# A gated mix of chunked attention and a SwiGLU network on one core: weight squares gathered in every third unit, block operands stored in pairs, the second half's operands elsewhere, and the first scan spread out

## The chip, the cores and the metric

The kernel is one launch on one core of a Trainium2 chip. The metric is device time in microseconds (us), the median of several executions. The core's engines run side by side, each with its own queue of instructions in program order: PE multiplies matrices (PEld loads its weights), DVE, ACT and POOL do elementwise work, and SP only issues DMAs. Every DMA of this kernel is issued by SP, in program order. An engine waits at an instruction until what it reads is written and until the buffer that it writes has been released by its last reader.

## The reference, cut

```python
x: [1, 2048, 576]                        # S = 2048 tokens, D = 576, 32 heads of 18, F = 4608
q, k, v = x @ wq, x @ wk, x @ wv         # four segments of 512 tokens
for s in range(4):                       # causal softmax attention inside the segment,
    a_dot = softmax(q_s @ k_s.T * 18 ** -0.5 + mask) @ v_s
    a_mem = (phi(q_s) @ M) / (phi(q_s) @ z + 1e-6)      # and a memory of the earlier ones
    o_s = sigmoid(beta) * a_mem + (1 - sigmoid(beta)) * a_dot
    M, z = M + phi(k_s).T @ v_s, z + phi(k_s).sum()
a = concat(o) @ wo
b = (silu(x @ w_gate) * (x @ w_up)) @ w_down
g = sigmoid((x * gate_w).sum(-1))
out = g * a + (1 - g) * b
```

All inputs and outputs are float32.

## The kernel before

**Two stages and a tail.** Stage one (0 to 234 us) computes q, k, v and the memory for the four segments: in each segment nine chains of matmuls for q and k (line 173), then eight v steps. Counted over the stage, chain n of segment s is step 17 s + n and v step n is step 17 s + 9 + n. Each chain has a list of small pieces of work for the other engines (`mid`), put between its matmuls. Stage two (234 to 1690 us) is the feed-forward network, with the attention's softmax woven in. The tail multiplies by `wo` and mixes.

**Units and beats.** Stage two runs over 72 units: half 0 is units 0 to 35 and half 1 is units 36 to 71. A half is half of the tokens (first segments 2 and 3, then 0 and 1), and a unit is one of 36 tiles of 128 of the 4608 columns, in both the gate and the up projection. The two projections of a unit are done in seven block products (a fast 2x2 block product that needs seven and not eight; `seven`, lines 1181 and 1184) whose operands are sums and differences of blocks of the weights and of x. Each operand is multiplied by a power of two and split into a float16 high part (by ACT, scale and copy) and a low part (by DVE, scale and subtract the high part): three products high x high, high x low, low x high. Line 1184 adds the last 64 rows of D, called the rest. ACT's copy at line 1249 takes the first product out of its bank. After the first four products there is one beat each, after the fifth also (beat 4), two after the sixth (beats 5 and 6), and one after the seventh (beat 7). `defer(k, fn)` puts a piece of work into the k-th beat from now; the work of one beat is issued in the order in which it was deferred.

**Long and short units.** The down projection (line 993) is done for three units together: with the first unit of each next three (units 3, 6, 9, ...) come sixteen groups of matmuls, spread over its beats together with the attention steps. These units are long (some 37 us of PE work); the others are short (10.6 us). An attention step is a generator (`att_gen`): it loads a row and four q and k stacks (lines 246 and 936), multiplies q and k for the row maxima (line 823, maxima at 830), later multiplies again and takes the exponential (lines 870 and 874), masks on POOL (882), rounds to float16 on DVE (960), takes the remainder on POOL (962) and multiplies with v (899, 901).

**Scales.** The power of two of x and of each group of four weight tiles comes from a scan of the data: `peak` on DVE (line 136, the largest square) or `square` on ACT (line 133, the sum of squares), one column of `sc` per tile; then `total` sums the columns, `power` turns them into a power of two, and `back` keeps its inverse. x and the first two weight groups are scanned in stage one: x in segment 0 (`scan`, `scan_step`), the 16 gate and up tiles of groups 0 and 1 in segment 1 (`look`), with the rests in segments 1 and 2. The other seven groups are scanned in half 0 by `glance`: a tile of 128x640 is loaded into a slot of x that half 1 will use, and squared by ACT eight beats later. Two or three glances belong to each of units 0 to 20, long or short; the last total and power come in unit 22.

**Weights.** `w_load` brings a unit's raw gate and up blocks two units ahead, in beats 2 and 5, into one of four buffers called raw (lines 252 to 257). `w_make` (297 to 324) makes the seven operands of the next unit: four sums on POOL (`total`), seven high parts on ACT (line 309), seven low parts on DVE (312), and seven stores (`keep`) to a DRAM tensor `wc`, from which half 1 fetches them (`w_fetch`).

**The second half's x.** Half 1 needs its own x operands: `rest_second` loads and splits the rest rows (DVE at line 199, ACT at 198) in units 30 and 31; `x_second` loads eight pieces of x, forms eight differences on POOL and makes fourteen splits (ACT line 129, DVE line 130), in the last two units of half 0 and in the ten beats behind them. The exponential and the silu need different tables on ACT: `exp_table` (lines 1174 and 1266) switches back, and the two silu instructions of a unit (lines 1274 and 1275 multiply with their results) switch to the other.

## Time and profile before

| What | Value |
|---|---|
| three runs | 1790.54, 1792.91, 1794.20 us (median 1792.91) |
| the profiled execution | 1789.5 us, of which the span is 1787.8 |
| granted clock of PE, mean over the span | 0.997 |
| PE busy | 1739.2 us (97%), 12401 matmuls |
| PE weight loads | 1228.8 us (overlap with PE) |
| DVE busy | 1359.4 us (76%) |
| ACT busy | 1021.7 us (57%) |
| POOL busy | 841.1 us (47%) |
| DMA | 290.21 MB, 162 GB/s on average |

The span runs from the first to the last instruction; the remaining 1.7 us lie around it. A busy time is the union of the instructions on an engine, in one profiled execution. In the rows by time, a row begins with its start and its duration in us, then engine, line and operation, output and inputs by the names of the program, shapes, and in brackets how long the engine stood idle before it and on what. In the rows by stretch, each engine has its busy time and, in brackets, its count of instructions. The share of a whole engine hides that the stages have different limits; the stretches are therefore cut at the starts of units, which are 234.2 (unit 0), 269.6 (3), 325.2 (6), 388.0 (9), 448.6 (12), 632.7 (21), 691.7 (24), 749.9 (27), 808.2 (30), 875.3 (33) and 955.6 us (36, the first of half 1).

### The profile page before, as it was taken

Reading aid. Unit: us, or ns where it says so; the run is one execution under the profiler, and the core shown is the slowest. Engines: PE = TensorE matmul, PEld = TensorE weight load, DVE = VectorE, ACT = ScalarE, POOL = GpSimd, SP = SyncE. Lnnn points to the kernel's source line nnn. Section 1 sums busy time; section 2 is a strip of 40 time slices with the busy share of each in tenths; the row PEclk is TensorE's granted clock in tenths of the full one; section 3 lists DMA queues with packets and bytes.
Section 4 is the critical chain, followed back from the end, with each engine's and each line's share of the span. In section 5 each row is a group of like instructions: output and inputs, shape, how many; then the busy total and the mean of one; then the engine's idle time right before and its main releaser. Section 6 shows DMA issues by size and latency. Waiting matters only on the chain.

```text
span 1787.8 us, 36760 instructions
## 1 busy us (share of the span) xinstructions
PE 1739.2 (97%) x12401; PEld 1228.8 (69%) x12401; DVE 1359.4 (76%) x3447; ACT 1021.7 (57%) x1848; POOL 841.1 (47%) x1065
## 2 busy tenths in 40 slices
PE   8999999999999999999999999999999999999999
PEld 6898856656755676666566757756766766766699
DVE  7678676778878878887877887778778778775455
ACT  6666585676577667655665555455455455465411
POOL 3335541345534544454444555555555555556121
PEclk9999999999999999999999999999999999999999
DMA  8745485775577555645555353354344344333544
GB/s 289 257 172 172 149 288 163 220 234 175 171 230 234 158 178 177 195 124 159 162 154 186 105 153 108 94 153 126 91 134 135 104 120 141 104 107 115 169 147 140
DMA packets 259933, 290.21 MB, mean 162 GB/s; under 512 B 91488, under 2 KB 204000, under 8 KB 259744
## 3 DMA queue, kind: packets, MB, share of 16 engines
q1 hardware_dynamic: 259744, 287.86, 52.0%
q8 instruction: 98, 1.61, 0.4%
q14 instruction: 91, 0.75, 0.2%
HBM read 189.94 MB, written 97.81 MB: 161 GB/s over the span
## 4 chain that ended last, share of the span: by engine, by line
PE 75%; DVE 9%; ACT 6%; DMA 5%; issue 4%; SPq 1%; POOL 1%; DVEq 0%; ACTq 0%; POOLq 0%
PE bank L1181 26%; PE bank L993 23%; PE bank L173 9%; PE bank L1184 4%; PE bank L870 4%; PE bank L823 4%; PE bank L899 2%; DMA xo<-in_wf_dram 1%; PE bank L901 1%; ACT xo L133 1%; DVE row L1274 1%; DVE row L1275 1%; DVE scr L830 1%; ACT bank L1249 1%; PE bank L481 1%
## 5 line engine op out<-in xcount | busy, mean ns | idle before, releaser
L993 PE MATMUL bank<-dw,hh 128*128 128x320 f32 (+1 forms) x2304 | 507.6, 313 | 7.0 <-DVE ya L1002 5.9
L962 POOL TENSOR_TENSOR p<-pe,p 128x512 f16<-128x512 f32 x320 | 380.1, 1188 | 183.1 <-DVE p L960 132.0
L993 PEld LDWEIGHTS bank<-dw,hh 128*128 128x128 f32 x2304 | 378.4, 189 | 33.2 <-DVE ya L1002 9.0
L874 ACT ACTIVATE pe<-bank 128x512 f32<-128x512 f32 x320 | 190.1, 594 | 338.6 <-PE bank L870 306.5
L993 PE MATMUL bank<-dw,hl 128*128 128x320 f32 (+1 forms) x1152 | 340.1, 295 | 0.2 <-DVE hl L126 0.2
L882 POOL TENSOR_SCALAR_AFFINE_SELECT pe<-pe 128x256 f32<-128x256 f32 (+1 forms) x320 | 146.0, 456 | 247.8 <-ACT pe L874 246.2
L830 DVE CUSTOM_DVE_ANT_0 scr<-bank,cm 128x512 bf16<-128x512 f32 (+3 forms) x512 | 247.6, 484 | 18.3 <-PE bank L823 9.3
L1002 DVE TENSOR_TENSOR ya<-bank,ya 128x320 f32<-128x320 f32 x352 | 156.6, 452 | 89.3 <-PE bank L993 86.9
L993 PEld LDWEIGHTS bank<-dw,hl 128*128 128x128 f32 x1152 | 217.6, 189 | 0.5 <-DVE hl L126 0.4
L1184 PE MATMUL bank<-xr,rh 128*128 128x512 f16 x504 | 191.3, 380 | 0.5 <-DMA rh<-rc 0.5
L870 PE MATMUL bank<-qst,kst 111*128 111x512 bf16 (+3 forms) x512 | 151.2, 303 | 0.0
L960 DVE CAST p<-pe 128x512 f16<-128x512 f32 x320 | 149.2, 467 | 0.0
L1092 DVE TENSOR_TENSOR hl<-row,hh 128x512 fp32r<-128x512 f32 x120 | 110.4, 920 | 26.0 <-ACT hh L1091 26.0
L823 PE MATMUL bank<-kst,qst 108*128 108x512 bf16 (+3 forms) x512 | 125.9, 299 | 2.5 <-ACT pe L874 1.3
L305 POOL TENSOR_TENSOR ws<-raw 128x256 f32<-128x256 f32 x72 | 64.1, 891 | 117.6 <-DMA raw<-in_wf_dram 45.1
L1259 ACT ACTIVATE row<-bank 128x512 f32<-128x512 f32 x72 | 43.1, 598 | 95.3 <-PE bank L1184 95.3
L1264 DVE TENSOR_TENSOR row<-bank,row 128x512 f32<-128x512 f32 x72 | 49.7, 690 | 58.4 <-ACT bank L1263 58.0
L173 PE MATMUL bank<-xo,qhi 128*128 128x512 f32 x288 | 91.4, 397 | 1.9 <-DVE ph L393 0.9
L1184 PEld LDWEIGHTS <-rh 128*128 128x128 f16 x504 | 49.3, 98 | 61.2 <-DMA rh<-rc 1.1
L1263 ACT ACTIVATE bank<-bank 128x512 f32<-128x512 f32 x72 | 41.9, 582 | 81.7 <-PE bank L1184 81.6
L391 POOL TENSOR_TENSOR q<-qr,q 128x512 bf16<-128x512 f32 x36 | 46.3, 1287 | 82.7 <-ACT q L390 74.1
L1274 DVE TENSOR_TENSOR row<-bank,row 128x512 f32<-128x512 f32 x72 | 49.7, 690 | 40.5 <-PE bank L1184 27.1
(1699 smaller groups left out, 3876.0 us busy)
## 6 DMA issues: line engine op xcount, KB each, us to landing
xo<-in_wf_dram SPq DMA_DIRECT2D x65, 320.0 KB
dc<-dw SPq DMA_DIRECT2D x36, 576.0 KB
dw<-dc SPq DMA_DIRECT2D x36, 576.0 KB
raw<-in_wf_dram SPq DMA_DIRECT2D x72, 256.0 KB
stk<-q SPq DMA_DIRECT2D x32, 384.0 KB
rh<-rc SPq DMA_DIRECT2D x72, 168.0 KB
draw<-in_wd_dram SPq DMA_DIRECT2D x36, 288.0 KB
vd<-vps SPq DMA_DIRECT2D x8, 912.0 KB
```

What stands on the lines that cost most here:

```text
L173: nc.tensor.matmul(t, st[n], mv[n], start=(n == 0), stop=(n == 13))
L823: nc.tensor.matmul(t[:, c:c + w], qs[:KR, pr, P * i:P * i + P], ks[:KR, pr, 0:w], start=True, stop=True)
L830: nc.vector.tensor_tensor_reduce(scr[:, :w], t[:, c:c + w], cm[:, L - w:L], 1.0, -3.0e38, OP.add, OP.max, m[:, k:k + 1])
L870: nc.tensor.matmul(t[:, c:c + w], ks[:KR + 3, pr, P * j:P * j + P], qs[:KR + 3, pr, P * j:L], start=True, stop=True)
L874: nc.scalar.activation(pe, t, AF.Exp, scale=SCALE)
L882: nc.gpsimd.affine_select(d, d, pattern=pat, compare_op=OP.is_ge, fill=0.0, base=0, channel_multiplier=-1)
L960: nc.vector.tensor_copy(p1, pe)
L962: nc.gpsimd.tensor_sub(p2, pe, p1)
L993: nc.tensor.matmul(t, p, q[:, cs], start=(f == CH * c and n == 0), stop=(f == CH * c + CH - 1 and n == 2))
L1002: nc.vector.tensor_add(ya[:, i, cs], t, ya[:, i, cs])
L1181: nc.tensor.matmul(t, w[:, p, z], x[z][:, q], start=first and n == 0, stop=False, skip_group_check=True)
L1184: nc.tensor.matmul(t, rem[:, RPOS[j]], XR[j], start=False, stop=True, skip_group_check=True)
```

## The change

- **Squares.** The eight glances of a weight group are all put in the unit that is a multiple of three (3, 6, ..., 21 for groups 2 to 8), loads in beats 0 to 5, squares in beats 2 to 7. Before, they were spread over three units. Scale and power follow in the next, short unit, as before.
- **Pairs.** The seven operands are kept in four tiles (0 with 3, 1 with 2, 4 with 5, 6 alone). ACT and DVE make both of a pair in one instruction of 128x512, and store and fetch go in four DMAs and not seven.
- **Second half's x.** `rest_second` begins in unit 24 and not 30, `x_second` in unit 27 and not 34, spread over units 27 to 33. Its pieces of x are loaded into the slots where operands will stand later, but for one (z = 1, q = 2), which takes a raw buffer.
- **First scan.** The scans of x and of the first two weight groups are spread over all chains of segments 0, 1 and 2 by two tables (`FETCH`, `GAUGE`). Five x tiles are no longer loaded for it: the high parts of segment 1's x are scanned where they stand, as those of segment 0 are. Segment 0 has 5 maxima on DVE (before: 20), segment 1 has 18 and 7 squares on ACT (9 and 8), segment 2 has 7 and one square (one maximum). The scales' totals and powers move behind them.

The diff, cut to its core:

```diff
-LOADS = ((-3, 0, 0), (-2, 0, 1), (3, 1, 0), (4, 1, 3), (4, 0, 3), (5, 0, 2), (5, 1, 1), (6, 1, 2))
-SUMS = ((2, 0, 1), (9, 0, 4), (10, 1, 1), (11, 1, 4), (13, 1, 2), (14, 1, 6), (17, 0, 2), (18, 0, 6))
-PARTS = ((1, 0, 0), (4, 0, 1), (10, 1, 0), (12, 1, 5), (12, 1, 3), (13, 1, 1), (14, 1, 2), (15, 1, 4), (16, 1, 6),
-         (16, 0, 5), (17, 0, 3), (18, 0, 2), (19, 0, 4), (20, 0, 6))
-FIRST = (9, 10, 11, 15, 16, 17, 18)
+FIRST = (9, 10, 15, 17)
+PAIR = ((0, 3), (1, 2), (4, 5), (6,))
...
-    wc = dram.tile([FT, 7, P, 4 * P], F16, name="wc")
+    wc = dram.tile([FT, 4, P, 8 * P], F16, name="wc")
...
-    def op_tile():
-        return wop.tile([P, 2, 2, P], F16, name="wo_")
+    def op_pair(ops, k):
+        n = len(PAIR[k])
+        t = wop.tile([P, 8 * P], F16, name="wo_")[:, :n * 4 * P]
+        v = t.rearrange("p (a b k n) -> p a b k n", a=2, b=n, n=P)
+        for b, j in enumerate(PAIR[k]):
+            ops[j] = v[:, :, b]
+        return t, t.rearrange("p (a n) -> p a n", a=2)
...
+        flat, both = [g.rearrange("p k n -> p (k n)"), None, None, a22.rearrange("p k n -> p (k n)")], {}
         def total(j, p, q, sub=True):
-            src[j] = rp.tile([P, 2, P], F32, name="ws", bufs=3)
+            k, b = divmod(j - 1, 3) if j < 4 else (1, j - 4)
+            if flat[1 + k] is None:
+                flat[1 + k] = rp.tile([P, 4 * P], F32, name="ws", bufs=2)
+            src[j] = flat[1 + k].rearrange("p (b k n) -> p b k n", b=2, n=P)[:, b]
...
-        def high(j):
-            ops[j] = op_tile()
-            nc.scalar.activation(ops[j][:, 0], src[j], AF.Copy, scale=sw[f // 4])
-        def low(j):
-            nc.vector.scalar_tensor_tensor(ops[j][:, 1], src[j], sw[f // 4], ops[j][:, 0], op0=OP.mult, op1=OP.subtract)
-        def keep(j):
-            nc.sync.dma_start(wc[f, j], ops[j].rearrange("p a k n -> p (a k n)"))
+        def high(k):
+            both[k] = op_pair(ops, k)
+            nc.scalar.activation(both[k][1][:, 0], flat[k], AF.Copy, scale=sw[f // 4])
+        def low(k):
+            hi, lo = (both[k][1][:, z] for z in range(2))
+            nc.vector.scalar_tensor_tensor(lo, flat[k], sw[f // 4], hi, op0=OP.mult, op1=OP.subtract)
+        def keep(k):
+            n = both[k][0].shape[1]
+            nc.sync.dma_start(wc[f, k, :, :n], both[k][0])
         todo = [(LEAD - 1, lambda: total(1, lambda: a21, lambda: a22, False)),
                 (LEAD, lambda: total(2, lambda: src[1], lambda: a11)),
                 (LEAD + 2, lambda: total(4, lambda: a11, lambda: a21)),
-                (LEAD + 4, lambda: total(5, lambda: a12, lambda: src[2]))]
-        for j in range(7):
-            todo += [(LEAD + j, lambda j=j: high(j)), (LEAD + j + 2, lambda j=j: low(j)),
-                     (LEAD + j + 3, lambda j=j: keep(j))]
+                (LEAD + 3, lambda: total(5, lambda: a12, lambda: src[2]))]
+        for k, o in enumerate((0, 1, 4, 6)):
+            todo += [(LEAD + o, lambda k=k: high(k)), (LEAD + o + 2, lambda k=k: low(k)),
+                     (LEAD + o + 3, lambda k=k: keep(k))]
...
         def b_sums(i):
-            a, b = rb[i], xr_tile(2 - 2 * i).rearrange("p (j n) -> p j n", n=P)
+            a, b = rb[i], xr_tile(2).rearrange("p (j n) -> p j n", n=P)
...
         def b_split(i, z):
...
-            both = xo.tile([P, 2, L], F16, name=f"xr{((3, 4), (3, 2))[i][z]}")
+            both = xo.tile([P, 2, L], F16, name=f"xr{((3, 0), (0, 1))[i][z]}")
...
-        ahead = [(f, u) for f in range(8) for u in range(2)]
         seen = {}
-        def look(n):
-            f, u = ahead[n]
-            seen[n] = xr_tile(1 + n % 6)
-            nc.sync.dma_start(seen[n].rearrange("p (k n) -> p k n", n=P), wf[f][:, u, 0:4])
-        def scan(k):
-            seen["x", k] = xr_tile(k % 7)
-            nc.sync.dma_start(seen["x", k], xT[1 + k // NT, :, k % NT])
+        def fetch(m):
+            seen[m] = xr_tile(2 + m % 5)
+            if m < 10:
+                nc.sync.dma_start(seen[m], xT[2 + m // NT, :, m % NT])
+            else:
+                f, u = divmod(m - 10, 2)
+                nc.sync.dma_start(seen[m].rearrange("p (k n) -> p k n", n=P), wf[f][:, u, 0:4])
+        def gauge(m, fn):
+            if m == "r0" or m == "r1":
+                i = int(m[1])
+                peak(rb[i].rearrange("p j n -> p (j n)"), 28 + 9 * i, junk)
+            elif isinstance(m, tuple):
+                s, kt = m
+                peak(f32(xs_of[s][0][kt][:, 0] if kt < 4 else xs_of[s][1]), NT * s + kt, junk)
+            else:
+                fn(seen.pop(m), 10 + m if m < 10 else 10 + m + (m - 10) // 8)
+        FETCH = (2, 3, 4, 5, 6, 7, 8, 9, 10, 11, 17, 18, 18, 19, 20, 20, 21, 22, 23, 26, 27, 28, 29, 30, 34, 35)
+        GAUGE = {4: (0,), 5: (1,), 6: (2,), 7: (3,), 8: (4,), 17: (5, 6, 7), 18: (8, (0, 0), 9), 19: ((0, 1), (0, 2), 10),
+                 20: ((0, 3), (0, 4), 11), 21: ((1, 0), (1, 1), 12), 22: ((1, 2), (1, 3), 13), 23: ((1, 4), 14, 15),
+                 24: (16, 17), 25: ("r0", 18), 34: (19, 20, 21), 35: (22, 23), 36: (24, "r1"), 37: (25,)}
         def scan_step(t):
-            r = []
-            for k in range(15):
-                at = 3 + k // 2 if k < 10 else k - 1
+            z = GAUGE.get(t, ())
+            return [lambda m=m, fn=(square if k == 2 else peak): gauge(m, fn) for k, m in enumerate(z)]
+        def scan_load(t):
+            for m, at in enumerate(FETCH):
                 if at == t:
-                    scan(k)
-                if at == t - 2:
-                    r.append(lambda k=k: peak(seen.pop(("x", k)), NT + k))
-            return r
+                    fetch(m)
+            if t in (21, 30):
+                b_load(t // 30)
...
-                if s == 0:
-                    if 1 <= n < 6:
-                        mid.append(lambda: peak(f32(xs_of[0][0][n - 1][:, 0] if n < 5 else xs_of[0][1]), n - 1, junk))
-                    mid += scan_step(n)
+                mid += scan_step(17 * s + n)
                 if s == 1:
-                    if n == 0:
+                    if n == 7:
                         mid.append(lambda: total(sx, 0, 20))
-                    if n == 2:
+                    if n == 8:
                         mid.append(lambda: power(sx, lone_tile([P, 1])))
-                    if n < 6:
-                        for k in range(2):
-                            look(2 * n + 4 + k)
-                    if n < 8:
-                        for k in range(2):
-                            c = 20 + 2 * n + k + n // 4
-                            mid.append(lambda c=c, k=k: (peak, square)[k](seen.pop(2 * n + k), c))
-                    if n in (5, 7):
-                        b_load((n - 5) // 2)
-                    if n == 7:
-                        mid.append(lambda: peak(rb[0].rearrange("p j n -> p (j n)"), 28, junk))
-                    if n == 8:
-                        mid.append(lambda: total(sw[0], 20, 29))
                 if s == 2:
-                    if n == 0:
-                        mid.append(lambda: peak(rb[1].rearrange("p j n -> p (j n)"), 37, junk))
-                    if n == 1:
-                        mid.append(lambda: total(sw[1], 29, 38))
-                    if n in (0, 2):
-                        mid.append(lambda: power(sw[n // 2], lone_tile([P, 1])))
-                        mid.append(lambda: back(n // 2))
+                    if n in (0, 4):
+                        mid.append(lambda: total(sw[n // 4], 20 + 9 * (n // 4), 29 + 9 * (n // 4)))
+                    if n in (2, 5):
+                        mid.append(lambda: power(sw[n // 4], lone_tile([P, 1])))
+                        mid.append(lambda: back(n // 4))
                     if n == 2:
...
-                    if n > 1 and blocks:
+                    if n > 2 and blocks:
                         mid.append(lambda z=blocks.pop(0): b_step(*z))
...
+                scan_load(17 * s + n)
...
-                if s == 0:
-                    for fn in scan_step(9 + n):
-                        fn()
-                    if n > 5:
-                        for k in range(2):
-                            look(2 * n - 12 + k)
+                scan_load(17 * s + 9 + n)
...
         def w_fetch(f):
...
-            def one(j):
-                ops[j] = op_tile()
-                nc.sync.dma_start(ops[j].rearrange("p a k n -> p (a k n)"), wc[f, j])
-            return [(j + 2 if f else FIRST[j], lambda j=j: one(j)) for j in range(7)]
+            def one(k):
+                t, _ = op_pair(ops, k)
+                nc.sync.dma_start(t, wc[f, k, :, :t.shape[1]])
+            return [((2, 3, 6, 8)[k] if f else FIRST[k], lambda k=k: one(k)) for k in range(4)]
...
         def x_second(new):
             r = {}
-            todo = []
+            done = []
             def load(z, q):
                 b, kt = ((0, z), (1, z), (0, 2 + z), (1, 2 + z))[q]
-                r[z, q] = wop.tile([P, L], F32, name=f"xq{q}", bufs=1) if z else raw_tile()[:, :L]
+                if z and q == 2:
+                    r[z, q] = raw_tile()
+                else:
+                    j = (0, 3, 4, 5)[q] if z == 0 else (2, 1, 0, 6)[q]
+                    x_home(1, j, 0)
+                    a, b_, _ = PLACE[1][j][0]
+                    r[z, q] = homes[a, b_][:, 2:4].rearrange("p a n -> p (a n)").bitcast(F32)
...
             def total(z, j):
...
-            todo += [(o, lambda z=z, q=q: load(z, q)) for o, z, q in LOADS]
-            todo += [(o, lambda z=z, j=j: parts(z, j)) for o, z, j in PARTS]
-            todo += [(o, lambda z=z, j=j: total(z, j)) for o, z, j in SUMS]
-            return sorted(todo, key=lambda t: t[0])
+            steps = [(3, 0, 0), (4, 1, 1), (4, 0, 5), (5, 1, 4), (6, 0, 4), (7, 0, 1), (8, 1, 2), (10, 0, 3), (12, 0, 2),
+                     (13, 1, 6), (17, 0, 6)]
+            todo = [(24 * z + q // 2, lambda z=z, q=q: load(z, q)) for z in range(2) for q in range(4)]
+            return todo + [(24 * z + o, lambda z=z, j=j, fn=(parts, total)[k]: fn(z, j)) for z in range(2) for o, k, j in steps]
         def rest_second(rest):
...
-            return [(0, load), (8, lambda: square(box[0], 20 + 9 * i + k))]
+            return [((0, 0, 1, 2, 3, 4, 4, 5)[k], load),
+                    ((2, 2, 3, 4, 5, 6, 6, 7)[k], lambda: square(box[0], 20 + 9 * i + k))]
...
-            i = 2 + pos // 3
-            if half == 0 and i < FT // 4:
-                for n in range(3 if pos % 3 < 2 else 2):
-                    plan += [(o + 3 * n - n // 2, fn) for o, fn in glance(i, 3 * (pos % 3) + n)]
-            if half == 0 and pos % 3 == 1 and pos > 3 and i <= FT // 4:
-                plan += [(1, lambda i=i: total(sw[i - 1], 11 + 9 * i, 19 + 9 * i)),
-                         (5, lambda i=i: power(sw[i - 1], ts_tile([P, 1]))), (6, lambda i=i: back(i - 1))]
-            if pos == FT - 6:
+            i = 1 + pos // 3
+            if half == 0 and pos % 3 == 0 and 2 <= i < FT // 4:
+                for k in range(8):
+                    plan += glance(i, k)
+            if half == 0 and pos % 3 == 1 and 2 <= i < FT // 4:
+                plan += [(1, lambda i=i: total(sw[i], 20 + 9 * i, 28 + 9 * i)),
+                         (5, lambda i=i: power(sw[i], ts_tile([P, 1]))), (6, lambda i=i: back(i))]
+            if pos == 24:
...
-            if pos == FT - 2:
+            if pos == 27:
...
-                plan += [(o + 8, fn) for o, fn in x_second(X2)]
+                plan += x_second(X2)
...
```

## The prediction

> **What bounds the kernel now.** I read the page first, then what the matrix engine waits for, then busy time cut at the unit starts, then the timelines of the stretches with idle time. The first row is from the page, the other three from the view of PE's waits (total us, times, longest).
>
> ```profile
> span 1787.8 us, 36760 instructions
> ...
> PE bank L1181 <- ACT bank L1249: 16.6, 16, 2.7
> ...
> PE bank L173 <- DVE vf L413: 4.2, 1, 4.2
> ...
> PE bank L173 <- DVE ph L393: 0.9, 1, 0.9
> ```
>
> PE does nearly all its work back to back in an order fixed by the program, so the time is that work plus PE's waits. Only a wait that ends can be gained. The largest group waits for ACT's copy at line 1249, the first ACT result that a unit needs. Where these waits lie is in the busy times by stretch (start and end, length, then PE, PEld, DVE, ACT, POOL busy, granted clock, DMA share, GB/s). The cuts are the starts of units 0, 3, 6, 9, 21, 24, 30, 33 and 36.
>
> ```profile
> 234.20:269.60 35.40, 32.56 (x148) 14.23 (x149) 25.91 (x53) 30.81 (x64) 13.20 (x20) 1.00 0.95 331
> 269.60:325.20 55.60, 53.71 (x308) 35.28 (x307) 38.29 (x98) 35.08 (x71) 10.14 (x13) 1.00 0.63 200
> 325.20:388.00 62.80, 57.99 (x321) 36.73 (x320) 46.48 (x114) 40.33 (x81) 22.60 (x33) 0.97 0.68 204
> 388.00:632.70 244.70, 234.13 (x1622) 154.55 (x1621) 201.83 (x488) 168.25 (x330) 122.63 (x169) 1.00 0.67 200
> 632.70:691.70 59.00, 58.08 (x407) 38.62 (x406) 47.59 (x121) 38.17 (x73) 29.55 (x39) 1.00 0.56 172
> 691.70:808.20 116.50, 116.12 (x808) 76.83 (x807) 94.26 (x228) 71.94 (x131) 58.33 (x77) 1.00 0.53 160
> 808.20:875.30 67.10, 59.28 (x405) 38.26 (x404) 55.63 (x121) 40.10 (x73) 36.17 (x43) 1.00 0.50 150
> 875.30:955.60 80.30, 77.97 (x548) 57.69 (x546) 64.75 (x142) 44.55 (x77) 35.59 (x39) 1.00 0.54 173
> ```
>
> Units 24 to 29 carry no weight squares and lose 116.50 - 116.12 = 0.4 us in six units: that is the floor. Units 0 to 23 lose 2.8 + 1.9 + 4.8 + 10.6 + 0.9 = 21.0 us, and 0.03 of 62.8 = 1.9 us more to the clock in units 6 to 8. Units 30 to 32 lose 7.8 us, 33 to 35 lose 2.3 us. Two short units, one with squares and one without, show the cause:
>
> ```profile
> 437.00:448.60 11.60, 10.69 (x50) 4.78 (x49) 9.01 (x17) 11.40 (x25) 3.83 (x5) 1.00 1.02 368
> 739.20:749.90 10.70, 10.65 (x50) 4.73 (x49) 8.39 (x14) 9.20 (x20) 3.63 (x5) 1.00 0.90 307
> ```
>
> ACT is full in the first (11.40 of 11.60 us) and has 1.5 us to spare in the second. In a short unit with squares ACT is the bound; in all others PE is.
>
> **The first scan.** These are PE's rows around the two waits of segment 0.
>
> ```profile
> 31.93 0.39 PE L173 MATMUL bank<-xs,qlo 128*128 128x512 f32 x1
> 33.20 0.70 PE L173 MATMUL bank<-xo,qhi 128*128 128x512 f32 x2 [0.87 <-DVE ph L393]
> ...
> 46.39 3.22 PE L173 MATMUL bank<-vw,xo 128*128 128x288 f32 x12 [4.17 <-DVE vf L413]
> ...
> 49.89 2.62 PE L173 MATMUL bank<-vw,xo 128*128 128x290 f32 x12
> ...
> 52.62 1.76 PE L173 MATMUL bank<-vw,xo 128*128 128x290 f32 x12
> ```
>
> After 4.17 us of idleness the same twelve matmuls take 3.22 and 2.62 us instead of 1.76: 1.46 + 0.86 = 2.3 us lost to the halved clock. The Trainium skill, "TensorE: Matmul & The Clock Gate", section "What's actually happening", has the clock fall to half after an idle window of about 3.4 us and come back after a busy one; the trace agrees here. The first two rows also show that a wait costs 0.17 us beyond its idle time: the starts are 1.27 us apart where the row's own spacing is about 0.23, and 1.04 is 0.17 over 0.87. DVE is late because of the scan's maxima:
>
> ```profile
> 42.67 0.68 DVE L136 CUSTOM_DVE_ANT_0 xr<-xr 128x512 f32<-128x512 f32 x1
> ...
> 43.28 1.63 DVE L136 CUSTOM_DVE_ANT_0 xr<-xr 128x512 f32<-128x512 f32 x1
> ```
> ```profile
> 42.81 1.54 POOL L391 TENSOR_TENSOR q<-qr,q 128x512 bf16<-128x512 f32 x1 [3.11 <-ACT q L390]
> ```
>
> Segment 0 goes from 20 maxima to 5: 15 x 0.68 to 15 x 1.63, so 10 to 24 us of DVE work leave a stretch where DVE was 5 us late. Both waits go, and the clock loss: 4.2 + 0.9 + 2.3 = **-7.4** (at least 4). The maxima come back later: segment 1 has 18 instead of 9 (squares 7 for 8), segment 2 has 7 instead of 1 and one square. DVE's room there:
>
> ```profile
> 58.20:97.50 39.30, 39.04 (x211) 33.56 (x210) 25.44 (x72) 28.77 (x63) 13.70 (x14) 1.00 0.79 276
> 115.60:144.00 28.40, 28.18 (x155) 24.24 (x155) 16.50 (x47) 18.81 (x36) 10.65 (x13) 1.00 0.52 179
> ```
>
> Nine more at 0.68 make 31.6 of 39.3 us, six more make 20.6 of 28.4: hidden behind PE. The weight-rest splits of segment 2 come one chain later, toward the first v steps, where PE already waits for DVE; one such split is 0.75 us (row below). Together **+1.0** (0 to 4). Five x loads of 256 KB less are hidden.
>
> **Squares in the long units.** Units 0 to 23 lose 22.9 us with the clock; the floor for 24 units is 1.6, so 21.3 can go. One square is
>
> ```profile
> L133 ACT ACTIVATE xo<-xo 128x640 f32<-128x640 f32 x56 | 40.6, 725 | 0.0
> ```
>
> and some 0.1 us more for its accumulator. A short unit sheds two to three, 1.7 to 2.5 us of ACT, more than the 0.9 us by which 11.60 exceeds 10.70: short units reach the floor, and long ones no longer start late. A long unit now takes eight: 5.8 us of ACT, where ACT has over 15 of 37 us idle. What is late next: the loads of squares 0 and 1 are issued in beat 0 and squared in beat 2, some 3 us later, while ACT can lose 3 us there before the next exponential is wanted; square 4 stands behind the two table loads and ahead of an exponential, 0.3 us more than the copy it replaces; and the eighth load stands in SP's queue ahead of four loads of q and k, as a square's load does now. I put back 0.7 us for each of the seven long units, 0.7 for unit 0 and 0.5 for unit 8: 6.1. Net **-15.2** (-8 to -20).
>
> **Paired block operands.** The rows are one old copy and one old subtraction, and the nearest ones of twice the size.
>
> ```profile
> 789.03 0.50 ACT L309 ACTIVATE wo__10388<-ws,sc 128x256 f16<-128x256 f32 x1
> ```
> ```profile
> 133.47 0.71 ACT L129 ACTIVATE xr<-xr,sc 128x512 f16<-128x512 f32 x1
> ```
> ```profile
> 770.53 0.48 DVE L312 SCALAR_TENSOR_TENSOR wo__9895<-raw,sc,wo__9895 128x256 f16<-128x256 f32 x1
> ...
> 134.21 0.75 DVE L130 SCALAR_TENSOR_TENSOR xr<-xr,sc,xr 128x512 f16<-128x512 f32 x1 [0.51 <-ACT xr L129]
> ```
>
> ACT per unit: 7 x 0.50 = 3.5 becomes 3 x 0.71 + 0.50 = 2.6. DVE: 3.4 becomes 2.7. SP issues three stores or fetches less. None of it is on PE's path once the squares are gone: **0** (-2 to +1), covered by PE. POOL's four sums stay; the second one is now wanted a beat earlier.
>
> **Second half's operands.** The rest terms move from units 30 and 31 to 24 and 25, on the same beats. Their first row waits for ACT, which is behind silu and two table loads, and DVE stands still:
>
> ```profile
> 833.21 0.74 DVE L199 SCALAR_TENSOR_TENSOR xr<-xo,sc,xr 32x512 f16<-32x512 f32 x1 [3.96 <-ACT xr L198]
> ```
> ```profile
> 834.47 0.51 PE L993 MATMUL bank<-dw,hh 128*128 128x256 f32 x2 [2.53 <-DVE ya L1002]
> ```
>
> That order stays, only 0.5 us of ACT ahead of it goes. I take 7.0 of the 7.8 us in the new place: **-0.8** (-4 to +1). The boundary at units 34 to 36 is freed of the x splits: **-2.0** of 2.3. These 14 splits go to units 27 to 32, five or so in a long unit: 4 x 0.75 us on a DVE that is busy 47 of 58 us per three units, with ACT ahead of each. **+2.2** (0 to 6).
>
> One load of x takes a buffer of the four that the raw weights rotate through, in unit 30. From then each weight load waits for a later release. The load for unit 32 at beat 5 now waits for POOL's last sum in beat 6, and SP issues in order: behind it stand the row and four q/k loads. In unit 27, which has the same beats, these rows stand (SP, then POOL, then PE):
>
> ```profile
> 770.75 0.66 SPq L257 DMA_DIRECT2D raw<-in_wf_dram  x1
> 771.46 0.30 SPq L246 DMA_DIRECT2D qst<-mxd  x1
> 771.80 0.77 SPq L936 DMA_DIRECT2D qst<-stk  x1
> ...
> 773.97 0.74 SPq L936 DMA_DIRECT2D kst<-stk  x1
> ```
> ```profile
> 778.02 1.27 POOL L962 TENSOR_TENSOR p<-pe,p 128x512 f16<-128x512 f32 x1 [1.35 <-PE bank L823]
> ```
> ```profile
> 780.48 0.38 PE L823 MATMUL bank<-kst,qst 108*128 108x512 bf16 x1
> ```
>
> The last PE row needs the last k load. That link shows in unit 6, by the chain in order of time and by PE's timeline:
>
> ```profile
> 353.10 2.28 DMA kst<-stk
> ```
> ```profile
> 355.51 0.38 PE L823 MATMUL bank<-kst,qst 108*128 108x512 bf16 x1 [0.50 <-DMA kst<-stk]
> ```
>
> In the frame of unit 27: POOL is free of beat 5 at 779.3, its sum ends near 780.0, the last k load is issued 773.97 - 770.75 = 3.2 us later and lands 2.3 us after that, at 785.5, against 780.5: 5.0 us. By the first scan's row such a stop costs about 1.6 us of clock more; a full busy window after the page's idle window would also be near that. **+6.6** (0 to 9). The next weight load but one waits until unit 32; late sums there: **+1.0**.
>
> **Sum.** -7.4 + 1.0 - 15.2 + 0 - 0.8 - 2.0 + 2.2 + 6.6 + 1.0 = -14.6. About 18 waits go on balance at 0.17 us each beyond their idle time: -3.1. So -17.7. The profiled execution took 1789.5 us (span 1787.8): 1771.8. The median of the runs is 1792.9, 3.4 above that execution and within their spread. I predict 1772.
>
> **Rivals.**
> - The k load is hidden (POOL's sum comes early enough, or the buffer is free by then): 1772 - 7.6 = 1764. For it: POOL has 2 us idle in that beat. Against: in-order POOL puts the sum behind the whole of beat 5.
> - DVE becomes the bound in segment 1. The row of 1.63 against 0.68 us shows a maximum slowed while POOL runs; if all nine added ones meet POOL, 25.4 + 9 x 1.63 = 40.1 us exceed the stretch's 39.3, and with the third segment's six some 5 us are lost: 1777. The Trainium skill, "GPSIMD Engine Reference", section "Key points", says that POOL shares its SBUF interfaces with VectorE instructions of two SBUF inputs; the trace agrees at 1.63 us. Against it: POOL runs only 13.7 of those 39.3 us.
> - The bunched loads come late: each long unit loses 2.5 us, 1.8 more than I put back, 12.6 in all: 1784. For it: 2.6 MB in one unit. Against: DMA is half idle there (0.53).
> - Slower: the eight loads hold up the q/k loads in every long unit as the weight load does in unit 30. SP stops at a load whose buffer waits for a square, the square waits for its own load, and PE stops 6.6 us seven times: 5.9 x 7 = 41 more, 1813. It decides from 17.7 / 7 + 0.7 = 3.2 us per long unit. Against: every reused buffer was squared at least a beat before.
>
> **How the numbers follow.** Forecast 0.55, k load hidden 0.2, DVE bound 0.09, late loads 0.1, slower 0.06. The forecast's own range is 1765 to 1779. The range 1758 to 1785 takes in the hidden k load with the squares' upper bound, and the late loads. A difference of 0.2% (3.6 us) is what a measurement of this kernel can tell: faster than 1789.3 is 0.91, same 0.03 (the late loads' far end), slower 0.06.
>
> **What would show it.** Right: waits for line 1249 nearly gone; short units at 10.6 to 10.8 us; no clock loss near 46 us; a new wait for q/k DMA in unit 30, with SP standing at the weight load; DVE waits for ACT in unit 24. Wrong: ACT full in the long units, squares waiting for DMA, PE waiting for DVE in the second segment, or unit 30 at 37 us.

## The result and the profile after

The changed kernel takes 1796.36 us (median of 11 runs, 1792.96 to 1798.32), the kernel before 1790.54 us in the same comparison (11 runs, 1789.17 to 1794.20). The ratio is 1.0028, 95% interval 1.0019 to 1.0038: slower by 5.8 us in the medians (some 5 us by the ratio), where 1772 and a gain were forecast. The profiled execution took 1797.75 us, its span 1795.8, 8.0 more than the profiled one of before.

First the span from the page of the changed kernel, then what PE waits for (total us, times, longest).

```profile
span 1795.8 us, 35846 instructions
```
```profile
PE bank L993 <- DVE ya L1002: 9.1, 7, 2.6
PE bank L1188 <- DVE bank L1263: 7.2, 6, 2.0
PE bank L823 <- DMA kst<-stk: 5.5, 4, 3.8
PE bank L1188 <- ACT bank L1256: 3.8, 4, 2.1
...
PE bank L139 <- DVE sc L136: 2.2, 1, 2.2
PE bank L170 <- DVE sc L140: 2.0, 1, 2.0
```

The large group of before, 16.6 us for ACT's first copy of a unit (now line 1256), is down to 3.8. In its place stand waits for DVE (`ya`, line 1263), for the k load, and two for the scale `sc`. The busy times by stretch, cut at the starts of the same units as before (0, 3, 6, 9, 21, 24, 27, 30, 33, 36), say where (start and end, length, then PE, PEld, DVE, ACT, POOL busy, granted clock, DMA share, GB/s):

```profile
238.00:272.00 34.00, 32.34 (x148) 14.36 (x149) 26.11 (x44) 26.57 (x48) 14.62 (x18) 1.00 0.82 281
272.00:326.00 54.00, 53.44 (x309) 35.32 (x308) 37.92 (x89) 34.12 (x62) 11.20 (x12) 1.00 0.60 205
326.00:387.20 61.20, 57.69 (x321) 36.71 (x320) 46.11 (x105) 38.92 (x71) 22.52 (x33) 0.97 0.67 205
387.20:621.60 234.40, 231.90 (x1621) 154.94 (x1620) 193.88 (x452) 162.44 (x293) 124.97 (x168) 1.00 0.69 212
621.60:679.80 58.20, 57.96 (x407) 38.77 (x406) 46.40 (x112) 40.04 (x73) 30.44 (x38) 1.00 0.63 202
679.80:748.00 68.20, 61.89 (x405) 40.06 (x404) 55.47 (x112) 38.53 (x64) 37.10 (x42) 0.95 0.50 154
748.00:811.40 63.40, 58.59 (x405) 38.43 (x404) 54.33 (x112) 38.84 (x64) 36.31 (x42) 1.00 0.52 162
811.40:885.00 73.60, 62.87 (x405) 40.07 (x404) 52.91 (x112) 38.79 (x64) 35.40 (x42) 0.93 0.46 144
885.00:962.80 77.80, 77.18 (x549) 57.72 (x548) 53.58 (x122) 35.63 (x58) 24.36 (x30) 1.00 0.42 144
```

| Stretch | before, us | after, us | difference | forecast |
|---|---|---|---|---|
| stage one | 234.2 | 238.0 | +3.8 | -6.4 |
| units 0 to 23 | 457.5 | 441.8 | -15.7 | -15.2 |
| units 24 to 32 | 183.6 | 205.2 | +21.6 | +9.0 |
| units 33 to 35 | 80.3 | 77.8 | -2.5 | -2.0 |

(The forecast's -3.1 for the waits themselves is not shared out.) The gain forecast for units 0 to 23 came, to half a microsecond; the short unit 11 takes 10.6 us and not 11.6, with ACT busy for 8.7 of them. But of these 15.7 us only 12.6 are idle time of PE; PE's busy time there falls by 3.1 (436.5 to 433.3), which is what the forecast had set apart for the waits. What the kernel loses against before lies in stage one and in the nine units to which the second half's operands were moved. Part of it is the clock behind PE's stops: the mean granted clock is 0.992 where it was 0.997, which over the two spans is some 9 us, PE's idle time included (an estimate from these two rounded figures).

**Stage one.** PE's and DVE's rows by time, in segment 0 and at the end of segment 1's chains:

```profile
42.40 1.82 PE L170 MATMUL bank<-vw,xo 128*128 128x288 f32 x12 [0.83 <-DVE vf L421]
...
90.66 0.35 PE L139 MATMUL bank<-sc 128*128 128x1 f32 x2 [2.21 <-DVE sc L136]
93.05 3.25 PE L170 MATMUL bank<-vw,xo 128*128 128x288 f32 x12 [2.04 <-DVE sc L140]
97.87 2.12 PE L170 MATMUL bank<-vw,xo 128*128 128x288 f32 x12
```
```profile
88.17 0.68 DVE L133 CUSTOM_DVE_ANT_0 xr<-xr 128x512 f32<-128x512 f32 x1
...
88.78 1.63 DVE L133 CUSTOM_DVE_ANT_0 xr<-xr 128x512 f32<-128x512 f32 x1
...
90.35 0.16 DVE L136 TENSOR_REDUCE sc<-sc 128x1 f32<-128x20 f32 x1
...
92.85 0.15 DVE L140 TENSOR_SCALAR sc<-bank 128x1 f32<-128x1 f32 x1
```

In the kernel before, the same first v step of segment 1 and the second stand here:

```profile
94.85 1.74 PE L173 MATMUL bank<-vw,xo 128*128 128x288 f32 x12
97.35 1.83 PE L173 MATMUL bank<-vw,xo 128*128 128x288 f32 x12
```

The wait of 4.17 us in segment 0 is 0.83, with no slow matmuls behind it, and PE arrives at the scale's product (line 139, a sum over partitions) at 90.66 - 2.21 = 88.45, 6.4 us ahead of the 94.85 at which it passes there before. There it stands: the total at 90.35 is behind two maxima, the read of the product at 92.85 behind two more (at 91.63 and 92.23), and the v step waits for that read of the product's bank. By the next v step PE is 97.87 - 97.35 = 0.5 us behind the kernel before: 6.9 us lost in one place, 4.25 of them idle, 0.35 the product itself and 2.3 the clock (3.25 us for twelve matmuls against 1.74).

**Unit 30.** SP, POOL, DVE and PE:

```profile
823.40 0.33 SPq L254 DMA_DIRECT2D raw<-in_wf_dram  x1
...
845.96 0.38 SPq L254 DMA_DIRECT2D raw<-in_wf_dram  x1
...
848.92 0.73 SPq L936 DMA_DIRECT2D kst<-stk  x1
```
```profile
844.77 1.17 POOL L311 TENSOR_TENSOR ws<-raw,ws 128x256 f32<-128x256 f32 x1
```
```profile
830.10 0.69 DVE L275 SCALAR_TENSOR_TENSOR rt<-rr,sc,rt 128x448 f16<-128x448 f32 x1 [1.77 <-DMA rc<-rt]
...
831.24 0.56 PE L993 MATMUL bank<-dw,hh 128*128 128x320 f32 x2 [2.56 <-DVE ya L1002]
...
851.31 0.58 PE L823 MATMUL bank<-kst,qst 108*128 108x512 bf16 x1 [3.80 <-DMA kst<-stk]
851.90 2.77 PE L1188 MATMUL bank<-xo,wo__10267 128*128 128x512 f16 x6
```

SP stands twice at a raw weight load, until 823.40 and until 845.96, right behind POOL's sum, which ends at 845.94. From there the last k load lands 851.31 - 845.94 = 5.4 us later. The first stop holds up the stores of the rest rows; DVE waits for them to overwrite their tile, and PE for DVE.

### The profile page after: what moved, and what is told of

Read it like the earlier page. It is cut to its first block, busy times and chain, and to the rows that moved or that the text cites. A ratio compares the mean times of both kernels' runs of the same rounds, so it can differ in the third digit from the quotient of the medians.

```text
span 1795.8 us, 35846 instructions
## 1 busy us (share of the span) xinstructions
PE 1745.5 (97%) x12401; PEld 1233.4 (69%) x12401; DVE 1347.3 (75%) x3339; ACT 1005.4 (56%) x1740; POOL 850.8 (47%) x1065
## 4 chain that ended last, share of the span: by engine, by line
PE 78%; DVE 7%; ACT 5%; issue 3%; DMA 3%; POOL 2%; SPq 1%; DVEq 0%; ACTq 0%; POOLq 0%
PE bank L1188 32%; PE bank L993 23%; PE bank L170 7%; PE bank L1191 5%; PE bank L823 4%; PE bank L870 4%; PE bank L899 2%; PE bank L901 1%; POOL q L399 1%; SPq L936 1%; DMA kst<-stk 1%; DMA rc<-rt 1%; ACT L1181 0%; DMA draw<-in_wd_dram 0%; DVE xo L127 0%
## 5 line engine op out<-in xcount | busy, mean ns | idle before, releaser
L993 PE MATMUL bank<-dw,hh 128*128 128x320 f32 (+1 forms) x2304 | 509.2, 313 | 10.1 <-DVE ya L1002 9.1
L962 POOL TENSOR_TENSOR p<-pe,p 128x512 f16<-128x512 f32 x320 | 386.0, 1206 | 168.7 <-DVE p L960 121.3
L993 PEld LDWEIGHTS bank<-dw,hh 128*128 128x128 f32 x2304 | 380.3, 190 | 35.1 <-DVE ya L1002 10.7
L960 DVE CAST p<-pe 128x512 f16<-128x512 f32 x320 | 152.8, 478 | 0.0
L1092 DVE TENSOR_TENSOR hl<-row,hh 128x512 fp32r<-128x512 f32 x120 | 114.8, 957 | 16.5 <-ACT hh L1091 16.5
```

The lines of the kernel that those rows point to most:

```text
L960: nc.vector.tensor_copy(p1, pe)
L962: nc.gpsimd.tensor_sub(p2, pe, p1)
L993: nc.tensor.matmul(t, p, q[:, cs], start=(f == CH * c and n == 0), stop=(f == CH * c + CH - 1 and n == 2))
```

## The experiments

The kernel before was run beside each: 1791.83 us in the first four, 1791.68 in the next four, 1791.67 in the last four. Unit lengths come from one profiled execution each. The kernel before is 1.1 to 1.3 us slower in these sets than in the first comparison, so a difference between kernels of different sets is good to about 1 us.

**1. The squares alone** (on the kernel before).

```diff
-            return [(0, load), (8, lambda: square(box[0], 20 + 9 * i + k))]
+            return [((0, 0, 1, 2, 3, 4, 4, 5)[k], load),
+                    ((2, 2, 3, 4, 5, 6, 6, 7)[k], lambda: square(box[0], 20 + 9 * i + k))]
...
-            i = 2 + pos // 3
...
+            i = 1 + pos // 3
+            if half == 0 and pos % 3 == 0 and 2 <= i < FT // 4:
+                for k in range(8):
+                    plan += glance(i, k)
...
```

> The kernel before with the weight squares alone moved into the long units. Theory: the squares' term stands by itself. In the changed kernel units 0 to 23 take 441.8 us where they took 457.5, so 1790.5 - 15.7 = 1775, with short units at 10.6 to 10.7 us. Rival: the gain needs the paired operands (ACT 3.5 us of copies per unit instead of 2.6); then the short units stay near 11.2 us and the total is about 1783.

1784.39 us, ratio 0.9951 (0.9936 to 0.9966). Units 0 to 23 take 448.2 us, the first row below, -9.3 and not -15.7: nearer the rival. Most short units reach 10.7 to 10.8 us; the long units 9 to 18 stay at 38.25 to 38.7 us. PE's row in unit 15 shows the longest of its waits there:

```profile
234.80:683.00 448.20, 434.19 (x2798) 279.18 (x2799) 359.03 (x874) 315.98 (x612) 198.66 (x270) 1.00 0.69 211
```
```profile
530.28 0.27 PE L823 MATMUL bank<-kst,qst 108*128 108x256 bf16 x1 [0.65 <-ACT pe L874]
```

An exponential stands behind a copy and a square, which stand behind a table load, and PE's next bank waits for it. That is 0.65 of the 1.4 us which this unit takes more than in the changed kernel; a wait of 0.5 us for `ya` is the next part.

**2. The first scan alone** (the stage-one part of the diff on the kernel before).

> The kernel before with the first scan alone spread over the chains. Theory: the gain of 6.4 us in segment 0 is taken back in segments 1 and 2, because PE itself computes the scales and waits there for DVE, which is behind the added maxima: stage one 3.8 us longer, 1794. Rival: the loss belongs to something else of the change; then stage one is 5 to 6 us shorter and the total is 1785.

1795.17 us, ratio 1.0016 (1.0006 to 1.0026). As the theory has it, if less: stage one takes 236.4 us, +2.2 and not +3.8, with the same two waits for `sc` of 2.2 and 2.0 us. The loss is the scan's own. (In the seven kernels of this study with the scan and the scales in these places, stage one takes 235.9 to 238.0 us; the changed kernel is the longest.)

**3. Totals and products elsewhere.**

```diff
+                if (s, n) == (2, 0):
+                    mid.append(lambda: total(sx, 0, 20))
+                if s == 2 and n in (0, 4):
+                    mid.append(lambda: total(sw[n // 4], 20 + 9 * (n // 4), 29 + 9 * (n // 4)))
                 mid += scan_step(17 * s + n)
-                if s == 1:
-                    if n == 7:
-                        mid.append(lambda: total(sx, 0, 20))
-                    if n == 8:
+                if s == 2:
+                    if n == 1:
                         mid.append(lambda: power(sx, lone_tile([P, 1])))
-                if s == 2:
-                    if n in (0, 4):
-                        mid.append(lambda: total(sw[n // 4], 20 + 9 * (n // 4), 29 + 9 * (n // 4)))
-                    if n in (2, 5):
+                    if n in (2, 6):
                         mid.append(lambda: power(sw[n // 4], lone_tile([P, 1])))
```

> The changed kernel; the totals of the scales stand ahead of the maxima of their step, the scale of x is computed in chain 1 of segment 2 and not in chain 8 of segment 1, that of the second weight group one chain later. All maxima stay where they are. Theory: PE's waits of 2.2 and 2.0 us near 91 us and the clock lost behind them (6.9 us in all by the matmuls' starts) vanish, and some 2 us of those near 130 and 144 us: 1796.4 - 8 = 1788. Rival: DVE as a whole is too slow for segments 1 and 2 with the added maxima; then PE waits for it at the v steps instead, and the total stays at 1794 to 1797.

1796.47 us: the rival's number, but in the main not its reason. The first v step of segment 1 starts at 87.80 us, so the stop there is gone; the waits came back in segment 2, at the transposes of the memory update (line 454), which use the bank that the product has just filled:

```profile
PE bank L454 <- DVE sc L140: 4.1, 2, 2.6
```

The rival's sign is there too, but smaller: the longest wait of a v step for DVE's `r` is 2.6 us, where it is 1.7 in the kernel before.

**4. A buffer of its own for the load of x.**

```diff
-                    r[z, q] = raw_tile()
+                    r[z, q] = wop.tile([P, L], F32, name="xq", bufs=1)
...
-                    accs[g] = ap.tile([P, 2, 8, E], F32, name="acc")
+                    accs[g] = ap.tile([P, 2, 8, E], F32, name="acc", bufs=1)
```

> The changed kernel with a buffer of its own for the one load of x that took a raw weight buffer in unit 30 (room for it comes from keeping one accumulator of the attention and not two). Theory: SP stands twice in unit 30 because the weight loads wait for that buffer; both waits of PE that follow (2.6 us for ya near 831 us, 3.8 us for the k load near 851 us) go with the clock behind them: unit 30 falls from 48.5 to about 39.5 us, 1787. Rival: the splits of x on ACT and DVE hold unit 30 up, and the k load only shows it; then unit 30 stays above 45 us, 1793 to 1796.

1785.53 us, ratio 0.9958 (0.9943 to 0.9973), 10.8 us less than the changed kernel. Unit 30 takes 38.7 us. The stretches of units 24 to 26, 27 to 29 and 30 to 32 are now

```profile
678.10:746.90 68.80, 61.96 (x405) 40.10 (x404) 55.03 (x112) 38.65 (x64) 38.14 (x42) 0.95 0.50 154
746.90:810.20 63.30, 58.53 (x404) 38.39 (x403) 54.05 (x112) 38.80 (x64) 36.08 (x42) 1.00 0.52 161
810.20:873.30 63.10, 58.56 (x405) 38.39 (x404) 52.94 (x112) 38.90 (x64) 36.53 (x42) 1.00 0.55 168
```

The last is 10.5 us shorter than the 73.6 of the changed kernel, the first two are not: the buffer was the cause of both stops in unit 30, and of nothing in the other two stretches.

**5. The products behind v steps** (`total` behind v step 0 of segment 1, `power` behind steps 3 and 6, the second group's total and product together in chain 6 of segment 2).

> The changed kernel; the scales of x and of the first weight group are totalled behind v step 0 of segment 1 and computed by PE behind v steps 3 and 6, where DVE has idle time (3.4 us at 97 us in the changed kernel), that of the second group in chain 6 of segment 2. The maxima stay where they are. Theory: what costs is PE computing a scale while DVE has a queue of maxima, and the one bank that the scale shares with the transposes of the memory update (they waited 4.1 us for it when the scale of x was moved to chain 1 of segment 2). Away from both, the 6.4 us of segment 0 are kept: stage one 230 to 232 us, 1789 to 1791. Rival: the nine and six added maxima make DVE the bound wherever the scales are; stage one stays at 235 us or more, 1795.

1795.36 us; stage one 235.1 us. The wait moved a second time; PE's product now waits for its total, and twice for DVE's last read of its bank at the v steps (1.8 and 1.5 us):

```profile
PE bank L139 <- DVE sc L136: 3.0, 1, 3.0
PE bank L139 <- DVE r L419: 1.8, 1, 1.8
```

**6. Single operands again** (experiment 4 with the seven copies, subtractions and stores of before).

> The changed kernel with a buffer of its own for the load of x, and with single block operands as before (seven copies, seven subtractions, seven stores). Theory after the run with the squares alone: each long unit from 9 to 21 lost 1.4 us with single operands (38.25 against 36.83 us), so the pairs are worth 5 x 1.4 + 1 = 8 us in units 0 to 23, and this kernel takes 1785.5 + 8 = 1793. Rival: the pairs matter only together with the place of the squares' loads in SP's queue; then it takes 1786 to 1788.

1797.02 us, 11.5 us more than experiment 4. Units 0 to 23 take 451.3 us where experiment 4 has 441.3. The pairs are worth about 10 us here, more than the theory's 8.

**7. x at units 33 to 36.**

```diff
-            todo = [(24 * z + q // 2, lambda z=z, q=q: load(z, q)) for z in range(2) for q in range(4)]
+            todo = [(4 + 12 * z + q // 2, lambda z=z, q=q: load(z, q)) for z in range(2) for q in range(4)]
...
-            if pos == 27:
+            if pos == 33:
```

> The changed kernel with the loads, differences and splits of the second half's x at units 33 to 36 and not 27 to 33; the load into a raw buffer then stands behind the last weight load. Theory: both SP waits of unit 30 are gone, units 27 to 32 fall from 137 us to some 127 (what is left is one copy of the half-sums), and the splits cost 2 to 4 us at the boundary: 1796.4 - 20 + 3 - 1 = 1779. The rest terms keep their 10 us in units 24 to 26. Rival: the splits cost the same wherever they are (5 us in units 27 to 29 and 5 in 30 to 32); then only the 10.8 us of the buffer are gained, 1786.

1786.35 us. Units 27 to 32 take 115.1 us, 21.9 less; the theory's sum has 20 for this, though its text stops at 127 us. But units 33 to 35 take 88.6 instead of 77.8. The splits, packed into four units, hold up the high part of the hidden values:

```profile
934.80 0.90 PE L993 MATMUL bank<-dw,hh 128*128 128x320 f32 x2 [4.05 <-ACT hh L122]
```

The theory's 2 to 4 us at the boundary was wrong by some 7; the total is the rival's.

**8. Low parts one beat later** (on experiment 4).

```diff
-            steps = [(3, 0, 0), (4, 1, 1), (4, 0, 5), (5, 1, 4), (6, 0, 4), (7, 0, 1), (8, 1, 2), (10, 0, 3), (12, 0, 2),
-                     (13, 1, 6), (17, 0, 6)]
+            steps = [(3, 0, 0), (4, 2, 0), (4, 1, 1), (4, 0, 5), (5, 2, 5), (5, 1, 4), (6, 0, 4), (7, 2, 4), (7, 0, 1),
+                     (8, 2, 1), (8, 1, 2), (10, 0, 3), (11, 2, 3), (12, 0, 2), (13, 2, 2), (13, 1, 6), (17, 0, 6), (18, 2, 6)]
...
+                if j >= 0:
+                    todo.append((6 + n, lambda j=j: rest_low2(rest[j], rr[SRC[j]])))
```

(In a step, 0 is now the high part, 2 the low one, 1 a difference; `rest_low2` is the subtraction of `rest_16`.)

> The changed kernel with a buffer of its own for the load of x, and the low parts of the second half's operands (rest terms and x) issued on DVE one beat after their high parts on ACT and not in the same beat. Theory: DVE stands behind ACT at these (5.9 us and 4.8 us in units 24 to 32 of the run with the own buffer) and PE waits in turn for DVE (15 us there); with a beat between them half of PE's loss goes, 1785.5 - 8 = 1777. Rival: the added DVE work itself, slowed while POOL runs (a subtraction of 1.71 us against 0.74), is the loss; then 1783 to 1787.

1779.54 us, ratio 0.9930 (0.9910 to 0.9950), 6.0 us less than experiment 4. Units 27 to 29 and 30 to 32:

```profile
747.10:807.30 60.20, 58.53 (x405) 38.41 (x404) 54.94 (x112) 38.60 (x64) 37.15 (x42) 1.00 0.53 167
807.30:867.20 59.90, 58.41 (x405) 38.33 (x404) 53.84 (x112) 38.59 (x64) 37.73 (x42) 1.00 0.57 177
```

DVE is as busy as in experiment 4 (54.9 and 53.8 us against 54.1 and 52.9) and the stretches are 3.1 and 3.2 us shorter. These 6.3 us were the order, not the work. Units 24 to 26, with the rest terms, fall from 68.8 to 65.0 us. The total falls by less than these 10.1 us, because units 0 to 23 and stage one take 4.0 us longer in this execution than in that of experiment 4, 2.9 of them in unit 8, where the edit changes nothing.

**9. Scales without PE's product.**

```diff
-        nc.tensor.matmul(t, one.to_broadcast([P, P]), out, start=True, stop=True)
+        if t is None:
+            t = out
+        else:
+            nc.tensor.matmul(t, one.to_broadcast([P, P]), out, start=True, stop=True)
...
-                        mid.append(lambda: power(sx, lone_tile([P, 1])))
+                        mid.append(lambda: power(sx, None))
...
-                        mid.append(lambda: power(sw[n // 4], lone_tile([P, 1])))
+                        mid.append(lambda: power(sw[n // 4], None))
```

> The changed kernel without PE's product in the three scales of stage one: each partition takes the scale from its own sum, so the sum over partitions is left out there. The maxima and their places are those of the changed kernel. Theory: PE's round trip to DVE for a scale is what cost the 6.9 us near 91 us and some 3 us near 125 and 144 us; without it stage one keeps the gain of segment 0 and takes 228 to 230 us instead of 236 to 238, 1788. Rival: DVE with the added maxima is the bound of segments 1 and 2; then PE waits for it at the v steps and stage one stays at 234 us or more, 1793 to 1796.

1786.94 us, ratio 0.9981 (0.9965 to 0.9997), 9.4 us less than the changed kernel. Stage one takes 229.4 us. All the maxima are where the change put them, and the first v step of segment 1 starts without a wait:

```profile
89.02 1.74 PE L173 MATMUL bank<-vw,xo 128*128 128x288 f32 x12
```

So most of the loss was PE's question to DVE, and not the maxima: 8.6 of the 238.0 us go with the products alone. Stage one is now 4.8 us shorter than before, where 6.4 were forecast; the longest wait of a v step for `r` is 2.2 us (1.7 before).

**10. Both products in chain 0 of segment 2.**

```diff
+                if (s, n) == (2, 0):
+                    for z in (sx, sw[0]):
+                        mid.append(lambda z=z: power(z, lone_tile([P, 1])))
+                    mid.append(lambda: back(0))
...
                 v_step(s, hf, i)
+                if (s, n) == (1, 0):
+                    total(sx, 0, 20)
+                    total(sw[0], 20, 29)
```

> The changed kernel with the totals of x and of the first weight group behind v step 0 of segment 1, both products on PE in chain 0 of segment 2, ahead of that step's maxima and of the transposes that share the bank, and the second group's in chain 6. Theory: with DVE's queue short at the start of segment 2 the products cost about 0.4 us each, as in the kernel before, and stage one takes 229 to 231 us, 1789. Rival: DVE is still behind there, and the wait moves once more: 235 us or more, 1795.

1793.77 us, ratio 1.0009 (0.9998 to 1.0021), and stage one 234.7 us: nearly the rival's. Two long waits are left, the second product for the first one's read of the bank, and a v step of segment 2 for `r`:

```profile
PE bank L170 <- DVE r L419: 2.9, 2, 2.6
PE bank L139 <- DVE sc L140: 1.9, 1, 1.9
```

At that v step DVE has come from a weight-rest split that took 2.91 us (at 152.35 us), one of those that the change put a chain later.

**11. Experiments 8 and 10 together.**

> The kernel with the own buffer and the later low parts (1779.5 us) with the scales placed as in the run before this one. Theory: the two add, 1779.5 - 7 = 1772.5. Rival: the wait for the scales moves once more: 1778 to 1780.

1772.38 us, ratio 0.9893 (0.9874 to 0.9912): the fastest kernel of the study, 19.3 us less than the kernel before. It is the theory's number, but in part by luck: the 7 us that the theory adds had not come in experiment 10, which gained 2.6. Stage one takes 237.5 us in experiment 8, 234.7 in experiment 10 and 232.3 here, with the scales in the same places as in experiment 10 and the same two long waits (1.9 and 2.6 us). What sets the two apart is the clock, which fell behind both waits there and behind neither here; the rows stand in the last section.

**12. Pairs with the squares where they were** (experiment 4 with the old places of the squares).

> The changed kernel with the own buffer, the paired operands kept, and the weight squares in the places of before. Theory: squares and pairs both relieve ACT; with pairs alone a short unit with squares needs 0.9 us less of ACT than the 11.40 of before and nearly fits its 10.7, so units 0 to 23 take some 449 us (before: 457.5; squares alone: 448.2; both: 441 to 445), 1785.5 + 6 = 1791.5. Rival: without moving the squares the pairs do nothing, 457 us, 1799.

1800.21 us, ratio 1.0046 (1.0030 to 1.0062): the rival. Units 0 to 23 take as long as in the kernel before:

```profile
236.50:694.40 457.90, 436.59 (x2798) 280.21 (x2799) 346.44 (x802) 300.38 (x543) 204.88 (x268) 0.99 0.64 206
```

ACT does 300.4 us there and 302.1 in the 441.3 us of experiment 4; the 16.6 us between the two are only a matter of where.

Unit 8 blurs all these comparisons of units 0 to 23. It takes 15.1 us in the kernel before and 12.1 to 17.2 in the others, because one stop of PE there lasts 1.4 to 3.6 us and the clock falls behind it or does not; no run was made on it. Without unit 8 the squares alone are worth 6.3 us (experiment 1), the pairs alone 1.4 (experiment 12), and both together 15.1 in the changed kernel and 13.3 in experiment 4.

## Why the prediction was wrong

- **Squares, -15.2.** Near in size (-15.7, of which 12.6 are the idle time that the term was made of), wrong in its make-up, so its agreement is partly luck. The squares alone give -9.3 (experiment 1). The rest is the pairs'. The -3.1 for the waits came: PE's busy time in these units falls by 3.1.
- **Pairs, 0, "covered by PE".** Wrong. Alone they give next to nothing (experiment 12, 457.9 against 457.5; 1.4 us without unit 8), so the cover that was named is there as long as the squares are spread out. With the squares moved, the eight squares stand in the long units ahead of exponentials that PE waits for, and the pairs are worth 6 to 10 us (448.2 - 441.8, and 451.3 - 441.3). In units 0 to 23 PE's waits for exponentials are 3.8 us with single operands (experiments 1 and 6) and 1.4 with pairs, those for ACT's first copy 5.9 and 6.4 against 3.4 and 4.0. That ACT's shorter copies do it is argued from these waits: the pairs also shorten DVE's subtractions and save stores, and no run separates these. I costed the two edits one by one; their product was the point.
- **First scan, -7.4.** Right in mechanism, 1.0 too large: 6.4 us gained by the end of segment 1's chains, clock loss included.
- **"Later scan +1.0, hidden behind PE".** This is the step that failed first: +10.2 was measured (3.8 + 6.4; by the shortest stage one with these places, 235.9 us, it is 8.1). I compared DVE's busy time with the length of the stretch, and experiment 9 says that this comparison was nearly right: without the products 1.6 of the 6.4 us are still lost. What I left out stands in the diff: totals and products move too, from a quiet place to right behind the maxima, and each product is a PE instruction that waits for DVE with all of PE's work queued behind it. The rival "DVE becomes the bound in segment 1" priced the same stretch at 5 us, but for a reason to which experiment 9 leaves at most these 1.6 us. Three other places for the products (experiments 3, 5 and 10) each met another wait, in all three at least in part for the product's bank.
- **Rest terms, -0.8.** They cost 10.0 us over the 58.25 of the floor in units 24 to 26, against 8.8 in units 30 to 32 of the kernel before: +1.1. Nothing was freed by the new place; in experiments 1 and 2, where they were not moved, units 30 to 32 take 68.3 and 68.5, also 10 over the floor. The 7.8 us that I split came from one execution.
- **x splits, +2.2.** Mis-sized: 5.1 us in units 27 to 29 (63.4) and 4.9 in units 30 to 32 (63.1 with the own buffer). I counted four subtractions per stretch on a DVE with room. But each stands in the same beat behind its copy on ACT, and DVE's order is fixed, so everything behind it waits too. A beat between the two removes 6.3 of the 10 us (experiment 8). What makes the rest is not shown. (With pairs, a stretch without splits takes 57.6 us, in experiment 7; by that floor the splits cost some 11 us.)
- **The k load in unit 30, +6.6, and late sums, +1.0.** The mechanism is as described and in its frame: 5.4 us from the sum to the landed load (5.5 worked out), a wait of 3.8 us (5.0), since PE itself came late. It cost 10.5 us in all (experiment 4), because the other weight load, at beat 2, stops SP as well; I had only the one at beat 5. The clock's part was put at 1.6 us by the first scan's row, but that row gives 2.3; in unit 30 PE is busy for 41.0 us where experiment 4 has 36.8, so the two stops cost 4.2 us of clock.
- **Boundary, -2.0.** Right: -2.5 in units 33 to 35.
- **Rivals.** ACT waited 15.7 us for late squares' loads, while PE's waits for k loads in units 0 to 23 only rose from 0.8 to 1.7 us, so the late loads and the held-up q/k loads did not come as priced. The sign "PE waiting for DVE in the second segment" did. None of the rivals had the signs of both losses.

The terms that failed make +9.2 (later scan) and +12.6 (units 24 to 32), 21.8 of the 24 us between forecast and result (25.7 by the two profiled spans).

## What to carry to other kernels

When an edit moves work from one engine to a later place, look for the instructions of the bound engine that wait for that work; the busy share of the moved engine does not show them. A buffer taken from a rotation is paid by the next users, and with one queue for all DMAs by everything queued behind them. Cost edits together when they relieve the same engine, and put a beat between the two halves of a split that runs over two engines.

## What was not expected of the hardware

The clock halved after shorter stops than the prediction's 4.17 us. Here are PE's and DVE's rows around a stop of 2.01 us in unit 25 of the changed kernel, and the stretches behind it, where the granted clock is 0.74, then 0.53, then full:

```profile
728.98 1.71 DVE L196 SCALAR_TENSOR_TENSOR xr<-xo,sc,xr 32x512 f16<-32x512 f32 x1
729.00 1.81 PE L1188 MATMUL bank<-xo,wo__9090 128*128 128x512 f16 x6 [2.01 <-DVE bank L1263]
...
731.04 2.62 PE L1188 MATMUL bank<-xo,wo__9090 128*128 128x512 f16 x6
...
733.71 1.46 PE L1188 MATMUL bank<-xo,wo__9204 128*128 128x512 f16 x6
```
```profile
729.00:731.00 2.00, 2.00 (x7) 0.78 (x7) 1.99 (x2) 0.00 (x0) 2.00 (x2) 0.74 0.18 68
731.00:733.50 2.50, 2.50 (x8) 0.89 (x7) 2.50 (x4) 2.14 (x4) 1.42 (x2) 0.53 0.00 0
733.50:735.00 1.50, 1.50 (x8) 0.68 (x7) 1.45 (x3) 1.49 (x2) 0.00 (x0) 1.00 0.58 124
```

Six matmuls take 2.62 us there and 1.46 at full clock. The Trainium skill, "TensorE: Matmul & The Clock Gate", section "What's actually happening", names an idle window of about 3.4 us; this trace has the loss after 2.01 us. This stop so costs nearly twice its length: unit 25 takes 14.4 us and not 10.6.

Not every such stop does. Experiments 10 and 11 have the same two stops in stage one: 1.9 us near 112 us, for a scale, and 2.6 us near 157 us, for `r`. In experiment 10 the granted clock falls behind both, in experiment 11 behind neither (experiment 10 first):

```profile
98.00:120.00 22.00, 20.10 (x124) 18.36 (x124) 16.59 (x54) 11.04 (x28) 5.51 (x7) 0.92 0.52 183
150.00:170.00 20.00, 17.41 (x123) 17.21 (x122) 18.62 (x44) 12.10 (x28) 9.80 (x13) 0.91 0.43 157
```
```profile
98.00:120.00 22.00, 20.10 (x131) 18.58 (x131) 17.32 (x56) 12.58 (x30) 5.51 (x7) 1.00 0.51 182
150.00:170.00 20.00, 17.43 (x135) 17.28 (x134) 19.03 (x47) 13.26 (x32) 9.21 (x12) 1.00 0.40 151
```

The stop of 2.53 us in unit 30 of the kernel before (PE's row at 834.47 us in the prediction) left the clock at 1.00 as well. In the clock records of all these traces the clock is halved for 3.41 or 6.83 us at a time. What decides whether it falls is not shown by these runs, so a stop of two microseconds is best priced both ways, with and without some 1.7 us (half of 3.41).

And the subtraction of line 196 takes 1.71 us at 728.98 us, with POOL busy for the whole 2.00 us of the stretch 729 to 731, against 0.74 at 734.06 us, in the stretch 733.5 to 735, where POOL has nothing to do.
